# A step of the weight decode is issued behind a slot's last first product, and in the last certain slot the first block's rows are read and normalized earlier

## The chip, the cores and the metric

One core of a Trainium2 chip runs the whole program. The metric is the device time of one execution in microseconds (us). Three runs of the kernel before took 1637.15, 1641.0 and 1641.97 us; their median is 1641.0 us.

## What is computed

Three parts follow each other: attention over keys and values pooled by eight, a mixture of eight experts with one expert per token, and a gated layer behind an RMS norm. Only the second and third matter here.

```python
logits = x @ w_gate                       # mixture: one expert per token
expert_idx = np.argmax(logits, axis=1)
h = np.maximum(xe @ w1[e], 0.0)           # xe: the tokens of expert e
out[mask] = gate_w[mask, None] * (h @ w2[e])
...
rms = np.sqrt(np.mean(x * x, axis=-1, keepdims=True) + 1e-06)
xn = x / rms * rms_g                      # gated layer
g = xn @ w_gate
silu = g * (1.0 / (1.0 + np.exp(-g)))
return (silu * (xn @ w_val)) @ w_out
```

There are 4608 tokens of width 512; an expert has 1024 hidden columns, the gated layer 1536. Its three weight matrices come as 64-bit floats, 18 *units* in all, each of two halves.

## The kernel before

**Slots.** Behind the attention the tokens are worked off in slots of 256 tokens of one expert (`body`, line numbers as in the profile). Slots 0 to 17 are certain to be needed; from slot 18 on each stands in a branch. A slot has two stages. Stage 1 (`stage1`, L572) makes eight first products, two to each of four PSUM banks `p_0` to `p_3`; behind each second one ScalarE rectifies the bank into `hh` (L575) and VectorE makes the remainder `hl` (L576). Then eight transposes (`xpose`, L605) prepare the tokens of the next slot, whose casts are L610 on ScalarE and L611 on VectorE. Stage 2 (`stage2`, L1058) makes the second products in one or two halves of 128 tokens: eight matmuls with `hh` and `w2h`, eight with `hh` and `w2l`, eight with `hl` and `w2h`. A half ends with the scaled result `ys` (L1069 or L1067), a sum of squares (L1070) and a store to `y_d` (L1073).

**New experts.** Where a slot begins a new expert, `change` and `change_half` split its weights within branches: `w2h` on ScalarE and `w2l` on VectorE (L149 and L150, 128x1024) behind the slot's first product, `w1h` and `w1l` (128x512) one slot earlier, one half of them behind the first product with number 4.

**The decode.** Beside the slots the 18 units are turned from 64-bit words into a high and a low 32-bit part. `unit_load` (L964) fetches a half of a unit into the tile `us`, of which there are two buffers. `unit_steps` gives the five steps of one half: step 1 a square on ScalarE (L983, it waits for the load and writes `ub`), step 2 (L986, L988), step 3 (L992, L994), step 4 (L997, L998) and step 5 (L1002) on VectorE.

**Order.** Nothing is scheduled automatically: each engine runs its instructions in the order in which the code issues them. The loop over the slots builds a table `fill` from places to steps, by `put_in`. Places 0 to 7 are behind the first product of that number, place 8 is behind the transposes and casts for the next slot, place 9 behind the first half of stage 2, place 10 behind the second. For slots 1 to 17 the five steps of a unit's first half stand at 2, 7, 7, 8, 8 and those of the second half at 9, 9, 10, 10, 10.

**The first block of the gated layer.** In slot 17 `ready` (place 8) reads the first 256 rows of `y_d` into a buffer of `us` (L1114); `norm_0` (place 10) normalizes them: a copy on GpSimd (L1141), two squares on ScalarE (L1139), twelve small steps on VectorE (L1120 to L1130) and two scalings (L1147). `turn_0` then transposes them on TensorE (L1155) ahead of slot 18, and ScalarE and VectorE take them out of PSUM (L1159, L1160).

Of the kernel before, what the change touches and what calls it, by code (L numbers as in the profile page):

```python
# [83 lines left out]
def fused(ctx: ExitStack, tc: tile.TileContext, q, k, v, moe_w_gate, moe_w1, moe_w2,  # L84
# [12 lines left out]
    NU = 18  # L97
# [502 lines left out]
    def xpose(s, c):  # L600

        px_ = px(c)
        for d in range(2):
            for z in range(2):
                nc.tensor.transpose(px_[:, d, 128 * z:128 * z + 128],  # L605
                                    xg[s][:, z, (2 * c + d) * 128:(2 * c + d) * 128 + 128], ident)
        if c and not s:
            nc.scalar.copy(out=lg0, in_=xg[0][:, :, DM:XW])
        hi, lo = (x[:, 2 * c:2 * c + 2] for x in xts[s])
        nc.scalar.copy(out=hi, in_=px_)  # L610
        nc.vector.tensor_tensor(out=lo, in0=px_, in1=hi, op=ALU.subtract)  # L611
        if c and s:
            gate_of(s)
# [347 lines left out]
    def unit_load(u, j):  # L961
        src, kk = unit_src(u, j)
        t = us_p.tile([128, 2 * DM + 2], I32 if wide else F32, tag="us", name="us")[:, 0:1024 if wide else 512]
        nc.sync.dma_start(out=t.rearrange("p (k n) -> p k n", k=kk), in_=src)  # L964
        ust[u, j] = t
# [41 lines left out]
    def unit_store(u):  # L1007
        if stored(u):
            for i, x in enumerate(held.pop(u)):
                nc.sync.dma_start(out=scr[u - EARLY, i], in_=x.bitcast(F32))  # L1010

    def gather(s):
        xg[s], xts[s] = xgs[s % 2], xhl[s % 2]
        for z in range(2):
            nc.gpsimd.indirect_dma_start(
                out=xg[s][:, z], out_offset=None, in_=x_d[:, :],
                in_offset=bass.IndirectOffsetOnAxis(ap=idx_g[:, z, s:s + 1], axis=0))
# [57 lines left out]
    def body(s, fill, f0=0):  # L1075

        last = s + 1 == NSLOT

        def put(place):
            for f in fill.get(place, ()):  # L1080
                f()

        for f in range(f0, 8):
            stage1(s, f)
            if f == 0 and s > 1:
                change(s, 1)
            if f == 4 and s and not last:
                change_half(s + 1, 0)
            put(f)
        if s and not last:  # L1090
            if s > 1:
                xpose(s + 1, 0)
                xpose(s + 1, 1)
            change(s + 1, 0)
            if s + 2 < NSLOT:
                gather(s + 2)
        xts.pop(s)
        put(8)
        soon(s + 1)
        stage2(s, 0, fill)  # L1100
        put(9)
        if s > 1:
            with tc.If(flag(s, HALF) > 0, preferred_fallthrough_block=True):
                stage2(s, 1)
        else:
            stage2(s, 1, fill)
        put(10)
# [99 lines left out]
    for s in range(SURE):  # L1207
        fill = {}

        def put_in(place, f):  # L1210
            fill.setdefault(place, []).append(f)

        if s == 0:
            for place, fs in tail.items():
                for f in fs:
                    put_in(place, f)
        if s == 1:
            put_in(0, lambda: gather(2))
            put_in((1, 2), lambda: xpose(2, 0))
            put_in((1, 3), lambda: xpose(2, 1))  # L1220
        for place, f in late:
            put_in(place, f)
        a = unit_steps(s, 0)
        b_ = unit_steps(s, 1)
        for place, f in zip((2, 7, 7, 8, 8) if s else [(0, 4)] * 5, a):
            put_in(place, f)
        if s + 1 < NU:
            put_in(9 if s else (0, 6), lambda s=s: unit_load(s + 1, 0))
        else:
            put_in(8, ready)  # L1230
        for place, f in zip((9, 9, 10, 10, 10) if s else [10] * 5, b_):
            put_in(place, f)
        if s + 1 == NU:
            put_in(10, norm_0)
        late = [(3, lambda s=s: unit_store(s))]
        if s + 1 < NU:
            late.append((3, lambda s=s: unit_load(s + 1, 1)))
        body(s, fill, 0 if s else 3)
        if s == 0:
            sctx.close()  # L1240
            vctx.close()
            psm = mctx.enter_context(tc.tile_pool(name="ps_m", bufs=1, space=PSUM))
            p1[:] = [psm.tile([128, 2, T], F32, name=f"p1_{i}") for i in range(4)]
# [187 lines left out]
```

## Time and profile before

| what | value |
|---|---|
| profiled execution, its own time | 1643.06 us |
| its span | 1641.3 us |
| median of three runs | 1641.0 us |
| TensorE busy, share of the span | 97% |
| VectorE / ScalarE / GpSimd busy | 51% / 30% / 16% |
| mean granted clock of TensorE | 0.983 |

The profiled execution's time is the span from its first to its last instruction and 1.8 us around it. The profile names TensorE PE (its weight loads PEld), VectorE DVE, ScalarE ACT, GpSimd POOL and SyncE SP; SPq is SP's issue of transfers. In a timeline a row has the start in us from the span's start, the length, engine, line, operation, the tiles and the count of merged instructions; a bracket gives the idle time of the engine ahead of the row and what ended it.

### The profile page before, as it was taken

The numbers are of one execution on the slowest core, as the hardware profiler recorded it, in microseconds if no ns is written. First come the engines' busy times: TensorE is split into PE (matmuls) and PEld (weight loads), VectorE is DVE, ScalarE is ACT, GpSimd is POOL, SyncE is SP. The second block draws the span as 40 slices with busy tenths as digits, with TensorE's granted clock in tenths as the row PEclk, the third lists the DMA queues.
The fourth block names the chain that finished last, engine by engine and source line by source line (L and its number), as shares of the span: only waits on it lengthen the run. The fifth ranks groups of instructions, "written<-read, shape, count | busy, mean of one in ns | idle before, by whom it ended". The sixth has DMA issues, their size and how long they took to land. (4 is left out here: it accounts for less than half of the span.)

```text
span 1641.3 us, 26444 instructions
## 1 busy us (share of the span) xinstructions
PE 1592.7 (97%) x9397; PEld 1377.7 (84%) x9399; DVE 836.6 (51%) x1717; ACT 488.9 (30%) x940; POOL 265.2 (16%) x362
## 2 busy tenths in 40 slices
PE   8999999999999998999999999999999999999997
PEld 6898889987998887889888888888888888888886
DVE  5688975778667785224433433334343333443222
ACT  3455633545334452222212112121211212122121
POOL 4687751011101110103000000000000000000000
PEclk9999999999999998999999999999999999999999
DMA  8977726486647464119201000010010001000000
GB/s 232 251 180 166 208 88 199 164 275 239 209 151 239 151 202 132 47 35 326 54 13 32 20 13 26 14 39 13 20 33 13 26 14 39 14 0 26 1 27 13
DMA packets 123515, 161.95 MB, mean 99 GB/s; under 512 B 36560, under 2 KB 85072, under 8 KB 123360
## 3 DMA queue, kind: packets, MB, share of 16 engines
q1 hardware_dynamic: 111328, 124.00, 26.1%
q0 software_dynamic: 11776, 35.91, 7.0%
q8 instruction: 77, 1.26, 0.3%
q14 instruction: 78, 0.64, 0.1%
q10 hardware_dynamic: 256, 0.13, 0.0%
HBM read 116.93 MB, written 43.08 MB: 97 GB/s over the span
## 5 line engine op out<-in xcount | busy, mean ns | idle before, releaser
L1328 DVE SCALAR_TENSOR_TENSOR th<-th,g 128x512 f32<-128x512 f32 (+1 forms) x120 | 76.1, 634 | 471.3 <-ACT th L1327 471.3
L1325 PE MATMUL g<-xh,rl 128*128 128x512 f32 (+1 forms) x576 | 217.3, 377 | 0.0
L1324 PE MATMUL g<-xl,rh 128*128 128x512 f32 (+1 forms) x576 | 217.3, 377 | 0.0
L1323 PE MATMUL g<-xh,rh 128*128 128x512 f32 (+1 forms) x576 | 217.2, 377 | 0.0
L1327 ACT ACTIVATE th<-g 128x512 f32<-128x512 f32 (+1 forms) x120 | 66.8, 557 | 463.4 <-PE g L1325 463.4
L1354 POOL DMA_INDIRECT out_dram<-o,tk x36 | 34.7, 965 | 815.7 <-ACT o L1353 788.9
L1349 PE MATMUL po<-rl,a 128*128 128x512 f32 x360 | 140.3, 390 | 1.6 <-DMA rl<-scr 1.6
L1348 PE MATMUL po<-rh,a 128*128 128x512 f32 x360 | 140.2, 389 | 0.0
L1350 PE MATMUL po<-rh,a 128*128 128x512 f32 x360 | 140.0, 389 | 0.0
L1323 PEld LDWEIGHTS g<-xh,rh 128*128 128x128 f32 x576 | 108.4, 188 | 20.3
L1324 PEld LDWEIGHTS g<-xl,rh 128*128 128x128 f32 x576 | 108.4, 188 | 20.3
L1325 PEld LDWEIGHTS g<-xh,rl 128*128 128x128 f32 x576 | 108.4, 188 | 19.9
L149 ACT CAST a<-th 128x512 fp32r<-128x512 f32 (+1 forms) x120 | 69.3, 578 | 167.2 <-DVE th L1329 167.2
L150 DVE TENSOR_TENSOR a<-th,a 128x512 fp32r<-128x512 f32 (+1 forms) x120 | 76.7, 639 | 77.3 <-ACT a L149 77.3
L1323 PE MATMUL g<-xh,uh 128*128 128x512 f32 (+1 forms) x288 | 108.7, 378 | 1.7 <-DVE th L1329 1.7
L1324 PE MATMUL g<-xl,uh 128*128 128x512 f32 (+1 forms) x288 | 108.6, 377 | 0.0
L1325 PE MATMUL g<-xh,ul 128*128 128x512 f32 (+1 forms) x288 | 108.6, 377 | 0.0
L572 PE MATMUL p<-xh,w1h 128*128 128x256 f32 x672 | 107.9, 283 | 0.6
L572 PE MATMUL p<-xh,w1l 128*128 128x256 f32 x672 | 106.9, 281 | 0.0
L572 PE MATMUL p<-xl,w1h 128*128 128x256 f32 x672 | 106.6, 280 | 0.0
L576 DVE SCALAR_TENSOR_TENSOR hl<-p,hh 128x512 fp32r<-128x512 f32 x84 | 56.9, 689 | 86.1 <-ACT hh L575 63.7
L572 PEld LDWEIGHTS p<-xh,w1h 128*128 128x128 f32 x672 | 92.7, 190 | 3.8 <-issue 1.1
(307 smaller groups left out, 3007.6 us busy)
## 6 DMA issues: line engine op xcount, KB each, us to landing
st<-in_moe_w_dram SPq DMA_DIRECT2D x64, 512.0 KB
y_d<-ys SPq DMA_DIRECT2D x39, 257.0 KB
v<-in_v_dram SPq DMA_DIRECT2D x32, 288.0 KB
y<-y_d SPq DMA_DIRECT2D x68, 128.0 KB
x_d<-x SPq DMA_DIRECT2D x16, 520.0 KB
k<-in_k_dram SPq DMA_DIRECT2D x16, 512.0 KB
q<-in_q_dram SPq DMA_DIRECT2D x14, 512.0 KB
scr<-uh SPq DMA_DIRECT2D x13, 512.0 KB
```

What stands on the lines that cost most here:

```text
L149: nc.scalar.copy(out=hi, in_=src)
L150: eng.tensor_tensor(out=lo, in0=src, in1=hi, op=ALU.subtract)
L572: nc.tensor.matmul(a, lhsT=w[d][:, fs], rhs=x[:, d], start=j + d == 0, stop=j == 2 and d == 3)
L576: nc.vector.scalar_tensor_tensor(out=lo, in0=bank, scalar=0.0, in1=hi, op0=ALU.max, op1=ALU.subtract)
L1323: nc.tensor.matmul(g[:, j], lhsT=wh[:, sl], rhs=hi[:, d], start=d == 0, stop=False)
L1324: nc.tensor.matmul(g[:, j], lhsT=wh[:, sl], rhs=lo[:, d], start=False, stop=False)
L1325: nc.tensor.matmul(g[:, j], lhsT=wl[:, sl], rhs=hi[:, d], start=False, stop=d == 3)
L1327: nc.scalar.activation(out=th, in_=g[:, 0], func=AF.Tanh, scale=0.5)
L1328: nc.vector.scalar_tensor_tensor(out=th, in0=th, scalar=1.0, in1=g[:, 0], op0=ALU.add, op1=ALU.mult)
L1348: nc.tensor.matmul(po, lhsT=a[:, 0, tsl], rhs=wh[:, sl], start=c == 0, stop=False)
L1349: nc.tensor.matmul(po, lhsT=a[:, 0, tsl], rhs=wl[:, sl], start=False, stop=False)
L1350: nc.tensor.matmul(po, lhsT=a[:, 1, tsl], rhs=wh[:, sl], start=False, stop=c == NC2 - 1)
```

## The change

In slots 1 to 16 step 1 of a unit's first half goes from place 2 to place 7. In slot 17 the first half's steps stand at places 2, 2, 3, 3, 3, the read of the first block at 4 and its norm at 9, ahead of what the second half has there; the second half's steps stand at 7, 7, 9, 9, 10.

```diff
-        for place, f in zip((2, 7, 7, 8, 8) if s else [(0, 4)] * 5, a):
+        end = s + 1 == NU
+        for place, f in zip((2, 2, 3, 3, 3) if end else (7, 7, 7, 8, 8) if s else [(0, 4)] * 5, a):
             put_in(place, f)
         if s + 1 < NU:
             put_in(9 if s else (0, 6), lambda s=s: unit_load(s + 1, 0))
         else:
-            put_in(8, ready)
-        for place, f in zip((9, 9, 10, 10, 10) if s else [10] * 5, b_):
+            put_in(4, ready)
+            put_in(9, norm_0)
+        for place, f in zip((7, 7, 9, 9, 10) if end else (9, 9, 10, 10, 10) if s else [10] * 5, b_):
             put_in(place, f)
-        if s + 1 == NU:
-            put_in(10, norm_0)
```

Three places show what it moves. The first is ScalarE in an ordinary slot, between the rectifications of the four banks. Before:

```order
L575 ACTIVATE hh<-p_0_3386 128x512
L983 ACTIVATE ub<-us 128x512
L575 ACTIVATE hh<-p_1_3387 128x512
L1023 TENSOR_LOAD row_i
L1027 COMPARE_AND_BRANCH
```

The square L983 stood behind the first bank's rectification. Now ScalarE has, at the end of the same slot's stage 1:

```order
L575 ACTIVATE hh<-p_2_3388 128x512
L575 ACTIVATE hh<-p_3_3389 128x512
L983 ACTIVATE ub<-us 128x512
L610 CAST xh_3109<-px 128x512 x2
L595 ACTIVATE gdf<-gdf 128x16
```

It stands behind the fourth bank and ahead of the casts for the next slot. The second place is VectorE at the end of slot 17. Before, the second half's steps 3 to 5 stood behind the slot's last scaling L1067, and the norm behind them:

```order
L1067 TENSOR_SCALAR ys_3120<-y,gates 128x512
L1103 UNCONDITIONAL_BRANCH x2
L992 SCALAR_TENSOR_TENSOR uh_9281<-ub,ua 128x512
L994 TENSOR_SCALAR ua<-uh_9281 128x512
L997 TENSOR_SCALAR ub<-us 128x512
L998 SCALAR_TENSOR_TENSOR ub<-us,ub 128x512
L1002 SCALAR_TENSOR_TENSOR ul_9282<-ub,ua 128x512
L1120 TENSOR_SCALAR nm_93<-nm_93 128x2
```

Now the norm's last small steps and its scalings L1147 come first:

```order
L1128 SCALAR_TENSOR_TENSOR nm_93<-nm_93 128x2
L1130 SCALAR_TENSOR_TENSOR nm_93<-nm_93 128x2
L1147 TENSOR_SCALAR y_9438<-y_9438,nm_93 128x512 x2
L992 SCALAR_TENSOR_TENSOR uh_9281<-ub,ua 128x512
L994 TENSOR_SCALAR ua<-uh_9281 128x512
L997 TENSOR_SCALAR ub<-us 128x512
L998 SCALAR_TENSOR_TENSOR ub<-us,ub 128x512
L1023 TENSOR_LOAD row_i
L1103 COMPARE_AND_BRANCH
L1067 TENSOR_SCALAR ys_3120<-y,gates 128x512
```

The norm went ahead of steps 3 to 5 and of the last scaling. The third place is ScalarE at the end of slot 17. Before:

```order
L1070 ACTIVATE y,ys_3119<-y,gates 128x512
L983 ACTIVATE ub<-us 128x512
L1023 TENSOR_LOAD row_i
L1103 COMPARE_AND_BRANCH
L1070 ACTIVATE y,ys_3120<-y,gates 128x512
L1103 UNCONDITIONAL_BRANCH x2
L1139 ACTIVATE sq_9673,nm_93<-y_9552 128x512
```

Now:

```order
L1069 ACTIVATE ys_3119<-y,gates 128x512
L1070 ACTIVATE y,ys_3119<-y,gates 128x512
L1139 ACTIVATE sq_9614,nm_93<-y_9438 128x512
L1139 ACTIVATE sq_9616,nm_93<-y_9438 128x512
L1023 TENSOR_LOAD row_i
L1103 COMPARE_AND_BRANCH
L1070 ACTIVATE y,ys_3120<-y,gates 128x512
```

The norm's two squares stand behind the first half instead of the second, and the square L983 of the second half has left this place.

## Rows read from the trace of the kernel before

**Rows 1.** The page's part 1: busy us (share of the span) xinstructions.

```profile
PE 1592.7 (97%) x9397; PEld 1377.7 (84%) x9399; DVE 836.6 (51%) x1717; ACT 488.9 (30%) x940; POOL 265.2 (16%) x362
```

**Rows 2.** Timeline of PE, slot 8, a slot without a stall.

```profile
408.23 0.63 PE L572 MATMUL p<-xh,w1h 128*128 128x256 f32 x4
...
419.43 1.03 PE L605 MATMUL px<-cc,both 128*128 128x128 f32 x8
420.22 2.11 PE L1058 MATMUL y<-w2h,hh 128*128 128x512 f32 x8
...
431.50 0.63 PE L572 MATMUL p<-xh,w1h 128*128 128x256 f32 x4
```

**Rows 3.** Timeline of PE, stage 2 of slot 5.

```profile
343.03 0.72 PE L1058 MATMUL y<-w2h,hh 128*128 128x512 f32 x2
346.65 2.99 PE L1058 MATMUL y<-w2h,hh 128*128 128x512 f32 x6 [2.90 <-ACTq L1027]
...
360.29 0.64 PE L572 MATMUL p<-xh,w1h 128*128 128x256 f32 x4
```

**Rows 4.** Timeline of PE, stage 2 of slot 7.

```profile
390.58 0.70 PE L1058 MATMUL y<-w2h,hh 128*128 128x512 f32 x2
...
395.65 2.07 PE L1058 MATMUL y<-w2h,hh 128*128 128x512 f32 x4 [1.83 <-ACT hh L575]
```

**Rows 5.** Timeline of PE, stage 2 of slot 12.

```profile
508.71 0.71 PE L1058 MATMUL y<-w2h,hh 128*128 128x512 f32 x2
511.32 0.73 PE L1058 MATMUL y<-w2h,hh 128*128 128x512 f32 x2 [1.90 <-ACTq L1027]
...
524.18 0.63 PE L572 MATMUL p<-xh,w1h 128*128 128x256 f32 x4
```

**Rows 6.** Timeline of PE, from the end of slot 17 through slot 18's stage 1.

```profile
643.94 2.12 PE L1155 MATMUL px<-cc,y 128*128 128x128 f32 x8 [6.56 <-issue]
...
658.90 1.04 PE L605 MATMUL px<-cc,both 128*128 128x128 f32 x8
```

**Rows 7.** Windows: length, busy us by engine, then PEclk, DMA share, GB/s.

```profile
345.90:352.70 6.80, 6.05 (x14) 4.57 (x15) 6.33 (x13) 2.75 (x6) 0.40 (x1) 0.50 0.99 296
...
209.00:216.00 7.00, 6.68 (x60) 6.69 (x61) 6.35 (x22) 2.20 (x5) 5.50 (x8) 1.00 0.20 79
```

**Rows 8.** Timeline of ACT, the squares of both unit halves in slot 5.

```profile
345.45 0.67 ACT L983 ACTIVATE ub<-us 128x512 f32<-128x512 f32 x1 [2.72 <-DMA us<-in_moe_w_gate_dram]
...
358.98 0.68 ACT L983 ACTIVATE ub<-us 128x512 f32<-128x512 f32 x1 [2.68 <-DMA us<-in_moe_w_val_dram]
```

**Rows 9.** Timeline of DVE, slot 5 (first two rows) and slot 7.

```profile
341.63 4.63 DVE L150 TENSOR_TENSOR w2l<-st,w2h 128x1024 fp32r<-128x1024 f32 x4 [0.35 <-ACT w2h L149]
346.17 1.28 DVE L576 SCALAR_TENSOR_TENSOR hl<-p,hh 128x512 fp32r<-128x512 f32 x2
...
387.24 4.63 DVE L150 TENSOR_TENSOR w2l<-st,w2h 128x1024 fp32r<-128x1024 f32 x4 [0.33 <-ACT w2h L149]
...
393.85 2.50 DVE L150 TENSOR_TENSOR w1l<-st,w1h 128x512 fp32r<-128x512 f32 x4
```

**Rows 10.** Timeline of PE, 209 us, a single wait.

```profile
209.32 1.73 PE L446 MATMUL av<-vbd,ptsb 96*128 96x146 f32 x12 [0.96 <-DVE x L477]
```

**Rows 11.** Timeline of several engines, end of slot 17.

```profile
633.02 0.20 ACT L1070 ACTIVATION_READ_ACCUMULATOR y<-y,gates 128x1 f32 x1
633.09 0.39 SPq L1114 DMA_DIRECT2D y<-y_d  x1
...
636.91 0.19 POOL L1141 COPY tk<-y 128x2 int32<-128x2 int32 x1 [15.58 <-DMA y<-y_d]
...
638.93 0.59 ACT L1139 ACTIVATE sq<-y 128x512 f32<-128x512 f32 x1
...
640.93 0.16 DVE L1120 TENSOR_SCALAR nm<-nm 128x2 f32<-128x2 f32 x1
...
643.35 0.89 DVE L1147 TENSOR_SCALAR y<-y,nm 128x512 f32<-128x512 f32 x2
```

## The prediction

> **What bounds the kernel.** I read the page first: TensorE is busy for 97% of the span, and no other engine for more than 51% [rows 1]. So a microsecond is won only where TensorE waits or where its clock is low. The waits of TensorE, listed with what ended them, are few; between 200 and 760 us the long ones that this change can touch are in stage 2 of slots 5, 7 and 12 and at the turn from slot 17 to slot 18. I then read TensorE's timeline there and held it against a slot without a stall.
>
> The measure is slot 8 [rows 2]. From its first product to its transposes it takes 419.43 - 408.23 = 11.20 us, the eight transposes take 0.79 us, and stage 2 with both halves takes 431.50 - 420.22 = 11.28 us, so 1.88 us for eight matmuls, 0.47 for two, 5.64 for a half.
>
> - Slot 5: 360.29 - 343.03 = 17.26 us [rows 3], 5.98 too many. The wait is 2.90 of it; the other 3.08 are clock: for 6.8 us behind the wait the granted clock is 0.50 [rows 7], 1.2 instead of 2.4 GHz.
> - Slot 7: from 390.58 [rows 4] to slot 8's first row at 408.23 [rows 2], 17.65 us, 6.37 too many, of which one wait is 1.83 [rows 4].
> - Slot 12: 524.18 - 508.71 = 15.47 us, 4.19 too many, with a wait of 1.90 [rows 5].
> - The turn: a wait of 6.56 us, then eight transposes and slot 18's stage 1 in 658.90 - 643.94 = 14.96 us [rows 6], where slot 8 needs 0.79 + 11.20 = 11.99, so 2.97 of low clock: 6.56 + 2.97 = 9.53.
>
> Together 5.98 + 6.37 + 4.19 + 9.53 = 26.07 us that TensorE loses there. The question is how much of it the change gives back.
>
> **Slots 5, 7 and 12.** All three begin a new expert. In slot 5 ScalarE, between the first and second rectification, is held for 2.72 us at the square L983, until the unit's load has landed at 345.45 [rows 8]; the three rectifications behind it are late, and TensorE, which already has the first two matmuls of stage 2 behind it, waits for them. With L983 behind the fourth rectification nothing that waits for a load stands ahead of them any more, and the wait goes. What is late next is VectorE, which must finish `w2l` and then make `hl`:
>
> - Slot 5: `w2l` ends at 341.63 + 4.63 = 346.26, four `hl` of 0.64 follow (1.28 for two) [rows 9], to 348.8; two matmuls and a half, 0.47 + 5.64, give 354.9. Without any wait stage 2 would end at 343.03 + 11.28 = 354.3. So 0.6 us stay.
> - Slot 7: the next slot begins a new expert too. `w2l` ends at 391.87, two `hl` 1.28, four `w1l` 2.50 [rows 9], two `hl` 1.28: 396.9; plus 0.47 and 5.64 is 403.0, against 390.58 + 11.28 = 401.9 without a wait. That leaves 1.2 if ScalarE and VectorE come forward with TensorE. They may not entirely: the load of slot 5's second unit half, for which ScalarE waits until 358.98 [rows 8], is issued behind the new expert's transfers and does not come forward. At worst the 5.4 us won in slot 5 are missing again in slot 7; at best nothing is. I take 0.4 of it, since there is a whole slot (slot 6) between for the two engines, which TensorE outlasts, to catch up: 1.6 us stay.
> - Slot 12: I have no row for its `hl`; what stays is between 0 and slot 5's 0.6. I take 0.3.
>
> The square itself costs nothing elsewhere: 0.67 us [rows 8] on an engine that is busy for 30%. But its wait now has other work behind it on ScalarE: the two casts L610 for the next slot, the gate's L595 and the scaling L1069. In slot 5 the load landed at 345.45, 3.2 us behind the last first product (343.03 - 0.79 = 342.24) [rows 3, 8]; the casts are wanted only when stage 2 is over, 11.28 us later or 5.64 in a slot with one half. In the 13 other slots from 1 to 16 TensorE loses little or nothing today at this place, so I cost the move at zero there, and the cover is that stage 2.
>
> Does the clock come back with the waits? At 209.32 TensorE had waited 0.96 us [rows 10], and over the 7 us from 209.0 the granted clock is 1.00 [rows 7]. The waits left here are single pieces of at most 0.8 us. I take it that the clock stays up.
>
> **The turn.** The read of the first block moves from behind the casts to place 4, behind the first half's decode, whose seven VectorE instructions are now ahead of the second `hl`; TensorE wants that `hl` only in the last third of the half, over 4 us after stage 1. The read took from 633.09 to 636.91, 3.8 us [rows 11]; issued some 7 us earlier it has landed when ScalarE is through with the first half at 633.2 (633.02 + 0.20) [rows 11]. SP's queue behind it holds the branch flags and the stores of stage 2, wanted later. Then: two squares, between 2 x 0.59 = 1.2 and 640.93 - 638.93 = 2.0; I take 1.5, as each is followed by the read of its sum: 634.7. Twelve small steps, 643.35 - 640.93 = 2.42: 637.1. Two scalings, 0.89 together: 637.6 and 638.0 [rows 11]. TensorE ends stage 2 at 643.94 - 6.56 = 637.38 [rows 6]. So the first transposes wait 0.2 us and those of the other 128 rows until 638.0: with the hand-overs 0.7 us stay of 9.53, and after so short a wait no clock is lost. Behind the norm, VectorE's scaling L1067 of the second half comes about 3 us later than today, and so the store and ScalarE's L1159; TensorE needs the PSUM banks of these only in slot 18's transposes and stage 2, 11 us on.
>
> **The sum.** Given back: 26.07 - (0.6 + 1.6 + 0.3 + 0.7) = 22.9 us. From slot 18 on everything moves forward as it is. The profiled execution took 1643.06 us, 0.13% above the median of 1641.0; against it the sum is 1620.2, and against the median **1618.1 us**.
>
> **Rivals.**
> - *Short waits still halve the clock.* Slot 5 keeps 0.6 us of waits, slot 7 1.6 us in three pieces. Each place that loses the clock again costs up to the 3.08 us of slot 5. For it: in slot 7 two waits in a row, each under 2 us, were enough. Against it: the 0.96 us at 209.32. One place gives 1621.2, all three of slot 5, slot 7 and the turn 1618.1 + 9.2 = 1627.3. The Trainium skill, "TensorE: Matmul & The Clock Gate", section "A second HAM failure mode: psum-queue depth-cycling", tells of a kernel whose clock swung although TensorE idled only briefly between groups of matmuls. By that rule this rival holds; the row at 209.0, with one wait and the full clock, does not bear it out.
> - *The second half's load comes late in slot 17.* Its L983 now stands ahead of the casts L610 and L1069; the trace says only that it had landed when ScalarE came to it, at the end of the first half. If it lands only then, the square, two casts and the gate push the squares back by some 2.5 us, the turn waits about 3 us and keeps its 2.97 us of low clock: 1618.1 + 5.2 = 1623.3.
> - *Only the turn is won.* If the three stalls are not the load's but come from ScalarE being late for other reasons, the change does not do there what it says: 9.53 - 0.7 = 8.8, so 1632.2. Against it: the row of L983 names the load [rows 8].
> - *Slower.* The square at place 7, held by its load, keeps the next slot's casts back, and TensorE stands at the next slot's first product. It decides where the load lands more than 5.64 - 2.4 = 3.2 us behind the last first product in a slot with one half, or 8.9 in one with two. To end at 1646, 22.9 + 4.9 us would have to be lost, 1.7 us in each of 16 slots. Slot 5, with its 3.2 us, is at the edge for a short slot, but it is a long one.
>
> **How the numbers follow.** A measurement of this kernel can tell about 0.3%, 4.9 us, from no change. The forecast has 0.60, the clock 0.20, the late load 0.08, the turn alone 0.05: all faster, 0.93 together. For a gain that is eaten up almost entirely, by several of these at once, 0.04; for slower 0.03. The range takes in the clock's rival, to 1627; at the low end all 26.07 us come back, 1614.9, and the runs before spread by 2 to 4 us: 1612. It leaves out the turn alone, no change and slower, 0.12 together.
>
> **What would show it.** In the profile of the changed kernel stage 2 of the three slots lasts 11.9, 12.9 and 11.6 us, the transposes L1155 wait under 1 us, and there is no window at clock 0.50 between 340 and 700 us. L983 stands behind the fourth rectification and still waits for its load in slot 5. Wrong would be a wait of TensorE ahead of a slot's first product, stage 2 of slot 7 above 15 us, or a wait of several us at L1155 for L1147.

## The result, and the profile after

The changed kernel takes 1619.85 us (median of 4 runs, 1618.34 to 1620.74); before, 1641.28 us (4 runs). The ratio is 0.9874, with an interval of 0.9856 to 0.9892. The profiled execution took 1619.92 us with a span of 1618.1, against 1643.06 and 1641.3: 23.2 us of span to account for.

On the page TensorE now works 98% of the span [rows 1]; its busy time fell by 10.3 us although its instructions are as many as before, so they ran faster.

```profile
PE 1582.4 (98%) x9397; PEld 1369.2 (85%) x9399; DVE 834.5 (52%) x1717; ACT 486.8 (30%) x940; POOL 263.2 (16%) x362
```

TensorE's timeline of the changed kernel, stage 2 of slots 5, 7 and 12 from its first row to the next slot's first product, answers to [rows 3 to 5]:

```profile
343.05 2.12 PE L1058 MATMUL y<-w2h,hh 128*128 128x512 f32 x8
...
354.34 0.64 PE L572 MATMUL p<-xh,w1h 128*128 128x256 f32 x4
...
385.42 2.11 PE L1058 MATMUL y<-w2h,hh 128*128 128x512 f32 x8
...
389.23 2.40 PE L1058 MATMUL y<-w2h,hl 128*128 128x512 f32 x8
392.24 2.13 PE L1058 MATMUL y<-w2h,hh 128*128 128x512 f32 x8 [0.60 <-issue]
...
397.93 0.63 PE L572 MATMUL p<-xh,w1h 128*128 128x256 f32 x4
...
497.96 2.12 PE L1058 MATMUL y<-w2h,hh 128*128 128x512 f32 x8
...
509.43 0.64 PE L572 MATMUL p<-xh,w1h 128*128 128x256 f32 x4
```

Where the wait of 2.90 us stood in slot 5, the eight matmuls follow each other. ScalarE's timeline of the same slot shows why: the fourth rectification is done when the square begins to wait, and the square still waits for its load, now 0.96 us [rows 8]:

```profile
342.08 1.09 ACT L575 ACTIVATE hh<-p 128x512 fp32r<-128x512 f32 x2 [0.32 <-ACTq L1027]
344.14 0.67 ACT L983 ACTIVATE ub<-us 128x512 f32<-128x512 f32 x1 [0.96 <-DMA us<-in_moe_w_gate_dram]
```

The end of slot 17, on several engines, answers to [rows 6, 11]:

```profile
611.82 0.39 SPq L1114 DMA_DIRECT2D y<-y_d  x1
613.90 0.67 ACT L983 ACTIVATE ub<-us 128x512 f32<-128x512 f32 x1 [1.87 <-DMA us<-in_moe_w_out_dram]
616.13 0.19 POOL L1141 COPY tk<-y 128x2 int32<-128x2 int32 x1 [11.27 <-DMA y<-y_d]
618.60 0.69 ACT L1069 ACTIVATE ys<-y,gates 128x512 f32<-128x512 f32 x1 [1.70 <-PE y L1058]
619.84 0.60 ACT L1139 ACTIVATE sq<-y 128x512 f32<-128x512 f32 x1
623.95 0.88 DVE L1147 TENSOR_SCALAR y<-y,nm 128x512 f32<-128x512 f32 x2
624.53 1.46 PE L1155 MATMUL px<-cc,y 128*128 128x128 f32 x8 [0.43 <-PE y L1058]
625.75 0.72 PE L572 MATMUL p<-xh,w1h 128*128 128x256 f32 x4
...
637.15 1.04 PE L605 MATMUL px<-cc,both 128*128 128x128 f32 x8
```

The block's rows have landed at 616.13, ScalarE squares them at 619.84, straight behind the first half's sum, and the transposes wait 0.43 us instead of 6.56. Windows over the places where the clock had fallen (length; busy us by engine; then PEclk, DMA share, GB/s) answer to [rows 7]. Before, in slots 7 and 12 and at the turn, the granted clock was 0.50:

```profile
393.70:400.50 6.80, 4.97 (x12) 3.80 (x12) 6.61 (x13) 3.35 (x7) 0.00 (x0) 0.50 1.04 395
513.20:516.60 3.40, 3.40 (x10) 2.62 (x9) 3.30 (x7) 0.44 (x1) 0.00 (x0) 0.50 0.78 260
639.50:649.70 10.20, 5.76 (x27) 5.61 (x28) 6.09 (x21) 2.65 (x8) 2.78 (x4) 0.50 0.70 145
```

After, it is 1.00 in all four places:

```profile
345.90:352.70 6.80, 6.80 (x30) 5.45 (x30) 5.37 (x13) 0.61 (x2) 0.98 (x1) 1.00 0.93 335
382.00:399.00 17.00, 16.40 (x90) 13.34 (x89) 15.82 (x29) 9.21 (x20) 4.16 (x4) 1.00 0.87 283
509.00:516.00 7.00, 7.00 (x59) 6.91 (x58) 5.86 (x10) 2.46 (x6) 0.41 (x2) 1.00 0.83 250
620.00:650.00 30.00, 29.57 (x184) 25.96 (x183) 13.28 (x36) 8.58 (x20) 4.21 (x6) 1.00 0.42 99
```

The account of the 23.2 us, each line from the start of a place to the next row behind it:

| place | before | after | won |
|---|---|---|---|
| up to slot 1's first product | 242.72 | 242.71 | 0.0 |
| slot 5, stage 2 | 17.26 | 354.34 - 343.05 = 11.29 | 5.97 |
| slot 7, stage 2 | 17.65 | 397.93 - 385.42 = 12.51 | 5.14 |
| slot 12, stage 2 | 15.47 | 509.43 - 497.96 = 11.47 | 4.00 |
| the turn, wait through slot 18's stage 1 | 6.56 + 14.96 = 21.52 | 0.43 + 637.15 - 624.53 = 13.05 | 8.47 |
| all else from slot 1 to slot 21's end | | | -1.77 |
| behind slot 21 | 905.07 | 903.69 | 1.38 |

Slot 21's end is the start of the next row less its wait, 736.23 before and 714.41 after, so that slots 1 to 21 took 493.51 and 471.70 us; what lies behind is the span less that end. TensorE's first row behind slot 21, before and then after:

```profile
739.80 0.58 PE L1323 MATMUL g<-y0t,uh 128*128 128x256 f32 x1 [3.57 <-ACTq L1244]
```

```profile
717.88 0.58 PE L1323 MATMUL g<-y0t,uh 128*128 128x256 f32 x1 [3.47 <-ACTq L1244]
```

The wait there is the same. The 1.38 us come from the clock behind it: the windows 737 to 747 before and 716 to 726 after have 0.66 and 0.83.

```profile
737.00:747.00 10.00, 7.20 (x40) 7.20 (x41) 0.84 (x2) 1.28 (x5) 3.80 (x8) 0.66 0.38 110
```

```profile
716.00:726.00 10.00, 8.12 (x57) 8.12 (x58) 1.65 (x4) 1.17 (x3) 4.72 (x9) 0.83 0.48 147
```

### The profile page after: what moved, and what is told of

It reads as the page before. It is cut to its first block, busy times and chain, and to the rows that moved or that the text cites. A ratio compares the mean times of both kernels' runs of the same rounds, so it can differ in the third digit from the quotient of the medians.

```text
span 1618.1 us, 26443 instructions
## 1 busy us (share of the span) xinstructions
PE 1582.4 (98%) x9397; PEld 1369.2 (85%) x9399; DVE 834.5 (52%) x1717; ACT 486.8 (30%) x940; POOL 263.2 (16%) x362
```

## The experiments

The experiments ran on three later occasions: the first four rows of the table on the first, the next four on the second, the last three on the third. The attention ahead of slot 1 then took 3 to 13 us longer than in the first two profiles, by an amount that changed from run to run, and the kernel before had medians of 1647.77, 1647.74 and 1644.59 us. So each kernel's time is held against before on its own occasion, and the traces by slots 1 to 21 alone, from slot 1's first product to slot 21's end as above. The kernel before, profiled once more on the third, gives 490.45 us. Each figure for the slots is from one profile, and two profiles of one kernel differ by up to 3 us. By them the change won 21.8 us in the slots the first time and 17.4 us later.

| kernel | median us | ratio to before | interval | slots 1 to 21, us |
|---|---|---|---|---|
| ordinary slots alone | 1635.07 | 0.9920 | 0.9899 to 0.9942 | 483.25 |
| slot 17 alone | 1640.60 | 0.9965 | 0.9948 to 0.9983 | 481.28 |
| square on other data | 1635.25 | 0.9926 | 0.9904 to 0.9949 | 478.98 |
| square at place 5 | 1630.53 | 0.9891 | 0.9867 to 0.9915 | 472.94 |
| the change again | 1628.72 | 0.9894 | 0.9860 to 0.9928 | 473.05 |
| second load first | 1626.30 | 0.9865 | 0.9835 to 0.9895 | 468.73 |
| before, filled | 1647.34 | 0.9997 | 0.9978 to 1.0017 | 485.80 |
| first load late | 1655.81 | 1.0043 | 1.0016 to 1.0069 | 499.81 |
| read early alone | 1633.18 | 0.9923 | 0.9900 to 0.9945 | 477.98 |
| norm early alone | 1629.33 | 0.9896 | 0.9872 to 0.9920 | 470.38 |
| second load first, again | 1623.88 | 0.9868 | 0.9845 to 0.9891 | 468.32 |

### The cause of the three stalls: the square on other data

The kernel before, but the square of a first half reads the bank that ScalarE has just rectified:

```diff
         def s1():
-            nc.scalar.activation(out=b_, in_=word(1).bitcast(F32), func=AF.Square)
+            src = word(1).bitcast(F32)
+            if j == 0 and u:
+                src = hh[:, 0:2].rearrange("p f t -> p (f t)").bitcast(F32)
+            nc.scalar.activation(out=b_, in_=src, func=AF.Square)
```

> The kernel before, with the square of each unit's first half at place 2 as it was, but reading the first rectified bank instead of the loaded words: same engine, place, size and output, no wait for the load. The decoded weights of the gated layer are then not the reference's. Theory (the wait for the load is the cause): the three stalls go though the order is unchanged; stage 2 of slots 5, 7 and 12 lasts at most 12.0, 13.1 and 12.1 us, 1626.3 to 1628.5 us in all. Rival (ScalarE is late there for other reasons, and the square's own 0.67 us or its place does it): waits of 1.8 to 2.9 us stay, and the time stays within 3 us of 1641.

Measured: stage 2 of slots 5, 7 and 12 lasts 11.28, 12.66 and 11.28 us. In slot 5, ScalarE (its square is L986 here) and TensorE (L1061) show:

```profile
349.94 0.63 ACT L986 ACTIVATE ub<-hh 128x512 f32<-128x512 f32 x1
350.48 0.58 ACT L575 ACTIVATE hh<-p 128x512 fp32r<-128x512 f32 x1
```

```profile
351.64 2.11 PE L1061 MATMUL y<-w2h,hh 128*128 128x512 f32 x8
```

The square stands where it stood before, runs as long, and costs nothing. What stalled TensorE was the wait for the load, not the square nor a late ScalarE. The rival is out. In time this kernel is 12.5 us below before, just short of the 12.8 to 15 us that the expected times stand for; the turn is as it was.

### How far it depends on the place: place 5

```diff
-        for place, f in zip((2, 2, 3, 3, 3) if end else (7, 7, 7, 8, 8) if s else [(0, 4)] * 5, a):
+        for place, f in zip((2, 2, 3, 3, 3) if end else (5, 7, 7, 8, 8) if s else [(0, 4)] * 5, a):
```

> The changed kernel with the square of slots 1 to 16 at place 5, behind the third rectification and ahead of the fourth. Theory (only what stands behind the square waits for the load): only the fourth bank is late. In slot 5 the load lands at 344.1 to 345.5, so the bank at 345.3 to 346.7, and TensorE wants it at 343.05 + 6 x 0.235 = 344.5: a wait of 0.9 to 2.2 us; in slot 12 about 0.2 us, in slot 7 none. If the clock falls only behind waits of over 1.8 us, 1620.5 to 1622 us; if also behind shorter ones, up to 1625. Rival (any square between the rectifications costs what it cost at place 2): stage 2 of the three slots is back at 17.3, 17.7 and 15.5 us, 1633 or more.

Measured in slot 5, on ScalarE and on TensorE:

```profile
355.52 0.67 ACT L983 ACTIVATE ub<-us 128x512 f32<-128x512 f32 x1 [1.81 <-DMA us<-in_moe_w_gate_dram]
```

```profile
356.72 0.73 PE L1058 MATMUL y<-w2h,hh 128*128 128x512 f32 x2 [1.25 <-ACT hh L575]
```

Six of the eight matmuls run, and the two that need the fourth bank wait 1.25 us, inside the expected 0.9 to 2.2. Slot 7 waits 0.58 and 0.71 us and slot 12 0.65 us, more than expected. Only what stands behind the square is late, and by the load's lateness less the lead that it has over TensorE. None of these waits brought the clock down (1.00 from 354 to 364, 396 to 412 and 510 to 525). The kernel is 17.2 us below before, the change, on the second occasion, 19.0.

### The two parts alone

Ordinary slots alone, with slot 17 as before:

```diff
-        for place, f in zip((2, 2, 3, 3, 3) if end else (7, 7, 7, 8, 8) if s else [(0, 4)] * 5, a):
+        for place, f in zip((2, 7, 7, 8, 8) if end else (7, 7, 7, 8, 8) if s else [(0, 4)] * 5, a):
...
-            put_in(4, ready)
-            put_in(9, norm_0)
+            put_in(8, ready)
...
-        for place, f in zip((7, 7, 9, 9, 10) if end else (9, 9, 10, 10, 10) if s else [10] * 5, b_):
+        for place, f in zip((9, 9, 10, 10, 10) if s else [10] * 5, b_):
...
+        if end:
+            put_in(10, norm_0)
```

> Only the square of slots 1 to 16 moves from place 2 to place 7; slot 17 and the turn are as before. Theory (the square's wait for its load held back the rectifications): the three stalls go, stage 2 of slots 5, 7 and 12 lasts 11.3, 12.5 and 11.5 us as in the changed kernel, the turn keeps its wait of over 6 us. The changed kernel won 5.97 + 4.90 + 4.09 = 14.96 us there and lost some 1.8 us in short waits of other slots, so 1626.3 to 1628.1 us. Rival (the gain of the slots is spent at the turn or depends on slot 17's part): the turn's wait grows by what the slots win, and the time stays above 1636.

Slot 17 alone, with the square of the others at place 2:

```diff
-        for place, f in zip((2, 2, 3, 3, 3) if end else (7, 7, 7, 8, 8) if s else [(0, 4)] * 5, a):
+        for place, f in zip((2, 2, 3, 3, 3) if end else (2, 7, 7, 8, 8) if s else [(0, 4)] * 5, a):
```

> Only slot 17 is changed; the square of slots 1 to 16 stays at place 2. Theory (the two parts are independent): the stalls of slots 5, 7 and 12 stay at 17.3, 17.7 and 15.5 us, the turn's wait falls to about 0.4 us with no low clock behind it: 8.6 us won there, 9.9 with the shorter stretch of low clock behind the last slot: 1631.4 to 1632.7 us. Rival (slot 17's gain needs the earlier loads that the other part brings): a wait of 2 us or more stays at the turn, and the time is 1635 or more.

Measured: 12.7 us and 7.2 us below the median of before, where 13.2 to 15 and 8.6 to 9.9 were expected. The turn behaved as expected both times: with the slots alone it waits 6.57 us, with slot 17 alone 0.29. Two things in the slots did not.

With the ordinary slots alone, slots 5 and 12 last 11.28 us in stage 2, but slot 7 lasts 14.93. ScalarE had been held for 5.71 us at the end of slot 5, by the load of the unit's *second* half, and TensorE waits in slot 7:

```profile
372.98 0.69 ACT L983 ACTIVATE ub<-us 128x512 f32<-128x512 f32 x1 [5.71 <-DMA us<-in_moe_w_val_dram]
```

```profile
402.01 1.22 PE L1058 MATMUL y<-w2h,hh 128*128 128x512 f32 x4 [1.56 <-ACT hh L575]
```

With slot 17 alone, stage 2 of slots 5 and 12 lasts only 15.88 and 13.87 us where it lasted 17.26 and 15.47. In slot 12 the wait was as long as before (1.85 us, before 1.90 [rows 5]), but the clock stayed up. TensorE's row and its window:

```profile
519.14 0.73 PE L1058 MATMUL y<-w2h,hh 128*128 128x512 f32 x2 [1.85 <-ACTq L1027]
```

```profile
517.00:524.00 7.00, 4.96 (x21) 3.41 (x20) 6.25 (x11) 3.21 (x6) 0.95 (x2) 1.00 0.90 270
```

### What slot 7 still loses: the second half's load

The change once more, and the change with the second half's load at the head of the slot. In SP's queue it then stands ahead of the weight transfers, and also ahead of the two stores of the unit before (L1010), which had come between them:

```diff
         for f in range(f0, 8):
             stage1(s, f)
+            if f == 0:
+                put("head")
             if f == 0 and s > 1:
                 change(s, 1)
...
-            late.append((3, lambda s=s: unit_load(s + 1, 1)))
+            late.append(("head" if s else 3, lambda s=s: unit_load(s + 1, 1)))
```

> The changed kernel once more, unedited, beside the other runs of this call. In the run with the ordinary slots' move alone, the attention ran some 12 us longer and transfers came later, and slot 7 lost 3.7 us again. Theory (the gain of slot 5 is partly handed back in slot 7 when the second half's load, issued behind the new expert's weights, comes late): where that load makes ScalarE wait over 4 us at the end of slot 5, stage 2 of slot 7 is over 14 us; where it waits 2.4 us as in the first profile, about 12.5. Slots 5 and 12 at 11.3 to 11.7 us and a turn with a wait under 0.7 us in either case; 21 to 23 us faster than before in the first case less 2 to 4. Rival (slot 7's loss belongs to the kernel with slot 17 unchanged): slot 7 at 12.5 us whatever the load does.

> The changed kernel with the load of each unit's second half issued at the head of its slot, ahead of the new expert's weight transfers on SP's queue, instead of behind the first product with number 3. Theory (the second half's late load makes ScalarE and VectorE late in slot 6 and so in slot 7): the square of the second half in slot 5 waits under 0.5 us for its load, stage 2 of slot 7 is at most 12.2 us, and the kernel is as fast as the change or up to 1 us faster where transfers are quick, 2 to 5 us faster where they are late. Rival (the weights are pushed back instead: the queue waits for the buffer of the second half before it can issue them, and the transfers collide): the splits L149 and L150 of a later slot begin later, TensorE waits at a first product or stage 2, and the kernel is 1 us or more slower than the change.

> The changed kernel with the load of each unit's second half at the head of its slot, once more, for its interval. From the first full slot to the end of slot 21 it took 468.7 us, against 471.7 and 473.1 in the two profiles of the change. Theory (the late load in slots 5 to 7 is what the change still loses there): 468.5 to 470 us again, stage 2 of slot 7 at 12.4 us or less, and a time against before of 0.984 to 0.988. Rival (the difference of 3 to 4.3 us was chance): 471 to 474 us, and a ratio of 0.988 or more.

Measured: in the repeat of the unedited change slot 7 lasts 14.57 us in stage 2, so what happened with the ordinary slots alone has nothing to do with slot 17. The second half's square in slot 5 and TensorE in slot 7, in the change again:

```profile
363.69 0.68 ACT L983 ACTIVATE ub<-us 128x512 f32<-128x512 f32 x1 [5.11 <-DMA us<-in_moe_w_val_dram]
```

```profile
392.72 1.23 PE L1058 MATMUL y<-w2h,hh 128*128 128x512 f32 x4 [1.54 <-ACT hh L575]
```

The same square with the load first, again: it no longer waits for its load at all, but 0.78 us for VectorE.

```profile
361.69 0.68 ACT L983 ACTIVATE ub<-us 128x512 f32<-128x512 f32 x1 [0.78 <-DVE ul L1002]
```

Over all kernels with the square at place 7 and the first half's load where the change has it, the second half's wait for its load in slot 5 and slot 7's stage 2 go together in two groups: waits of 2.38, 2.54 and 3.56 us (the change, read early, norm early) with 12.51, 11.91 and 12.06; waits of 5.11 and 5.71 with 14.57 and 14.93. With the load first, stage 2 of slot 7 lasts 12.35 us, a little over the expected 12.2, and then 11.73. That the earlier load undoes slot 7's loss rests on one pair, 14.57 against 12.35 on the second occasion: on the third, read early and norm early lose little there without it, and the loss of the first profile had other parts. What delayed the load, the weights or the two stores, was not separated.

Slots 1 to 21 take 468.73 and 468.32 us, less than any other kernel here, 3.0 to 4.7 us less than the two profiles of the change and 2.1 us less than norm early alone on the same occasion. Against the repeat most of it is in slot 7; against the first profile it is in slots 6, 13 and 16. Against before the ratios are 0.9865 and 0.9868, and those of the change 0.9874 the first time and 0.9894 on the second occasion: lower twice, but with intervals that overlap. So the gain over the change stands in two traces against two, and is not shown by the times. The rival (the weights are pushed back) is not seen: slots 5 and 12 stay at 11.28 to 11.35.

### What the clock costs: filling the waits

The kernel before, with matmuls of zeros where TensorE waited:

```diff
         for n in range(24):
+            for _ in range({(5, 2): 12, (7, 2): 7, (7, 4): 7, (12, 2): 8}.get((s, n), 0) if z == 0 else 0):
+                nc.tensor.matmul(y, lhsT=ones, rhs=zero.unsqueeze(1).to_broadcast([128, 64, 8]), start=False, stop=False)
...
+            px_ = px(c)
+            for _ in range(0 if c else 29):
+                nc.tensor.matmul(px_.rearrange("p a b -> p (a b)"), lhsT=ones, rhs=zero.unsqueeze(1).to_broadcast([128, 64, 8]))
```

> The kernel before, with matmuls of zeros put into TensorE's stream at the four stalls (12, 14 and 8 in stage 2 of slots 5, 7 and 12, 29 ahead of the turn's transposes), somewhat shorter than the waits; nothing else is moved. Theory (about half of what the stalls cost is the clock that falls behind the wait): the waits' length stays but the clock stays at 1.00 in all four places: 3.1 us less in slot 5, 2.7 in slot 7, 2.1 in slot 12 and 3.0 at the turn, 10.9 us in all less than before. Rival (the clock falls for another reason than the idle engine, or zeros do not count): windows at clock 0.50 stay in these places and the time is within 2 us of before.

> The kernel before, unedited, for a profile beside the others of these calls, whose times of before were some 6 us above the first ones. Theory (the extra lies in the attention, whose transfers come later in these calls, and the loss in the slots is as it was): the first full slot starts some 8 us later than the 242.7 of the first profile, and from there to the end of slot 21 it takes 490 to 494 us, 21 to 24 more than the change. Rival (the stalls of before are smaller in these calls, since the clock does not fall behind each wait): 483 to 488 us, the waits as long as before but fewer windows at clock 0.50.

Measured: the time is that of before, 0.9997. The clock did what was expected; windows over slot 5 and over the turn, in before once more and then in the filled kernel:

```profile
354.00:364.00 10.00, 6.25 (x17) 4.61 (x17) 7.89 (x14) 3.24 (x7) 0.50 (x2) 0.66 0.75 246
...
645.00:663.00 18.00, 11.43 (x78) 11.20 (x78) 9.53 (x26) 5.09 (x12) 2.77 (x4) 0.81 0.58 120
```

```profile
354.00:364.00 10.00, 9.80 (x44) 6.23 (x43) 8.32 (x16) 3.42 (x7) 1.18 (x2) 1.00 0.90 290
...
642.00:660.00 18.00, 17.62 (x122) 13.56 (x121) 10.06 (x27) 5.70 (x13) 2.78 (x5) 1.00 0.58 119
```

But the gain was mis-sized. Before, once more, already lost less than in the first profile (its 490.45 us are 17.4 and 18.8 more than the two profiles of the change, where 21 to 24 was expected): stage 2 of slots 7 and 12 lasted 16.30 and 12.74 us, and behind the wait of 0.71 in slot 12 no clock was lost. Against it the filled kernel wins 3.32 us in slot 5, 1.39 in slot 7 and 1.89 over slots 17 and 18, loses 1.06 in slot 12, where the zeros take 1.91 us and the wait was 0.71, and 0.9 in other slots: 4.65 us over slots 1 to 21. Behind slot 21 it loses 2.05 again (907.03 against 904.98 us), where the longest wait within the gated layer is 3.12 instead of 1.74 us; why was not tried. Filling keeps the clock; the change, which removes the waits, is worth 12.8 to 14.1 us more in the same slots (485.80 against 473.05 and 471.70).

### How much the new place covers: the first half's load late

```diff
-            put_in(9 if s else (0, 6), lambda s=s: unit_load(s + 1, 0))
+            if not 0 < s < NU - 2:
+                put_in(9 if s else (0, 6), lambda s=s: unit_load(s + 1, 0))
...
+            if 0 < s < NU - 2:
+                late.append((2, lambda s=s: unit_load(s + 1, 0)))
```

> The changed kernel with the load of each unit's first half, in slots 2 to 16, issued in the slot itself behind the first product with number 2 instead of in the slot before behind the first half of stage 2. Theory (the square at place 7 holds back only the next slot's casts, so it may be late by stage 2 less 2.4 us of casts and gate: 8.9 us behind the last first product in a slot with two halves, 3.2 with one): in slots without weight transfers the load is issued 7 to 8 us ahead of the square and costs nothing; in slots with them (4, 5, 7, 8, 12, 15) it lands up to 10 us late, and TensorE waits at the next slot's first product, 2 to 7 us behind slots 4 and 15, under 3 us behind the others: 4 to 14 us slower than the change. Rival (the place covers any lateness, since stage 2 needs nothing of it): within 1.5 us of the change. The other side (a late square hurts as it did at place 2): waits in stage 2 of the same slot and over 20 us slower.

Measured: 27.1 us slower than the change on the same occasion (1655.81 against 1628.72), and slower than before. ScalarE and TensorE at the end of slot 4, which has one half:

```profile
343.60 0.67 ACT L983 ACTIVATE ub<-us 128x512 f32<-128x512 f32 x1 [8.10 <-DMA us<-in_moe_w_gate_dram]
344.17 1.06 ACT L610 CAST xh<-px 128x512 fp32r<-128x512 f32 x2
```

```profile
344.80 1.00 PE L572 MATMUL p<-xh,w1h 128*128 128x256 f32 x4 [3.51 <-ACT xh L610]
```

The mechanism is the one expected: the wait is at the next slot's first product, behind slots 4, 8 and 15, and stage 2 of slot 5 is untouched at 11.29. The size was low: behind each of the three waits, of 3.51, 3.23 and 3.28 us, the clock falls (0.79 in 344 to 360, 0.80 in 445 to 462, 0.77 in 610 to 630), and slots 5, 9 and 16, which follow them, become 4.38, 6.31 and 4.53 us longer than in the change again, on top of the waits (slot 9 also has a second wait of 1.28). It also gives the cover. TensorE could have begun at 344.80 - 3.51 = 341.29; the first product came 1.20 us after the landing; stage 1 ended at 334.65. So a load may land 341.29 - 1.20 - 334.65 = 5.4 us behind the last first product in a slot with one half. In the changed kernel slot 5's load, of the first halves the one for which the square waited longest, landed 344.14 - 342.26 = 1.9 us behind it.

### The turn: read early or norm early

Read early alone puts the norm back to place 10; norm early alone puts the read back to place 8:

```diff
             put_in(4, ready)
-            put_in(9, norm_0)
...
+        if end:
+            put_in(10, norm_0)
```

```diff
-            put_in(4, ready)
+            put_in(8, ready)
             put_in(9, norm_0)
```

> The changed kernel with the norm at place 10 again, behind both halves; the read stays at place 4. Theory (the turn's wait is the norm's chain behind the second half, not the read): the read lands over 10 us before it is wanted, and the turn still waits 5.5 to 6.6 us, with up to 3 us of low clock behind it: 5.5 to 9.5 us slower than the change. Rival (the read was the bound): the turn waits under 3 us, and the kernel is less than 4 us slower than the change.

> The changed kernel with the read at place 8 again, behind the casts for the next slot; the norm stays at place 9. In the kernel before the read was issued at 633.09, just when VectorE's last use of the buffer (L998) ended. Theory (what freed the read is the decode's earlier end, not its own place): the read is issued at the end of stage 1, some 1 to 2 us later than in the change, lands at least 3 us before ScalarE's squares, and the turn waits under 0.7 us: within 1 us of the change. Rival (the place of the read counts): it is issued behind the first half of stage 2, the squares wait for it, and the turn waits 2 us or more: 2 to 6 us slower than the change.

Measured with the read early alone, on ScalarE and TensorE:

```profile
627.13 0.59 ACT L1139 ACTIVATE sq<-y 128x512 f32<-128x512 f32 x1
...
631.58 2.12 PE L1155 MATMUL px<-cc,y 128*128 128x128 f32 x8 [6.00 <-issue]
```

and with the norm early alone, on SP, GpSimd, ScalarE and TensorE:

```profile
622.05 0.39 SPq L1114 DMA_DIRECT2D y<-y_d  x1
625.84 0.19 POOL L1141 COPY tk<-y 128x2 int32<-128x2 int32 x1 [12.05 <-DMA y<-y_d]
...
628.19 0.60 ACT L1139 ACTIVATE sq<-y 128x512 f32<-128x512 f32 x1
...
632.67 1.46 PE L1155 MATMUL px<-cc,y 128*128 128x128 f32 x8 [0.21 <-PE y L1058]
```

With the read early alone the turn waits 6.00 us and slots 1 to 21 take 7.6 us more than with the norm early alone (477.98 against 470.38), and 6.3 and 4.9 us more than in the two profiles of the change, where 5.5 to 9.5 was expected. The medians, 1633.18 and 1629.33, differ by less, since the time outside the slots differs too: slot 1 begins at 245.66 and 252.16 us. With the norm early alone the turn waits 0.21 us, no more than in the change, and the read has landed 2.35 us before the squares, a little less than the 3 expected. So the read's own place is worth nothing here. The buffer is free in time: VectorE's last use of it (L998) ends at 619.91, and the read is issued at 622.05, where before it was held until 633.09. That the decode's steps at 2, 2, 3, 3, 3 do this follows from the order; they were not put back by themselves.

## Why the prediction was right, step by step

The forecast was 1618.1 us; measured were 1619.85, and in the profiled execution 1619.92 against a forecast of 1620.2. Its main cause and its places are shown by the runs; the sum is right to some extent by luck, because errors cancel (+0.7 in the four places, -1.8 in the other slots, +1.4 behind them), and on the second occasion the same change gave 19.0 us instead of 21.4.

- **Slot 5** (0.6 us were to stay): nothing stayed, 11.29 against 11.28. The step that failed took the end of `w2l`, 346.26, as fixed. VectorE came forward as well: in the changed kernel, on VectorE, the split begins at 339.74, not at 341.63 [rows 9], and the first `hl` stand at 344.28.

```profile
339.74 4.62 DVE L150 TENSOR_TENSOR w2l<-st,w2h 128x1024 fp32r<-128x1024 f32 x4
344.28 1.28 DVE L576 SCALAR_TENSOR_TENSOR hl<-p,hh 128x512 fp32r<-128x512 f32 x2
```

- **Slot 7** (1.6 were to stay): 12.51 - 11.28 = 1.23. The bounds from nothing to 5.4 us missing again were the right worry: in two other runs, with the second half's load later, 3.3 and 3.7 us are missing. The pieces were not as told: `w1l` ahead of the last `hl` costs 2.40 - 2.03 = 0.37, and the wait of 0.60 ahead of the second half has no engine as its releaser.
- **Slot 12** (0.3): 0.19. **The turn** (0.7): 0.43 of wait, 0.43 more in the transposes (1.22 instead of 0.79) and 0.20 in stage 1 (11.40 instead of 11.20), 1.06 in all. Given back in the four places: 23.58, predicted 22.9.
- **The move costs nothing elsewhere**: this term failed by 1.77 us. Slots 6, 13 and 16 became 0.55, 0.68 and 0.90 longer, slot 9 0.33 shorter. In slot 16 the second half's load comes in again: in the first profile its square was held for 2.85 us in slot 15 and slot 16's stage 2 lasted 12.46 us, in the repeat it did not wait for that load and stage 2 lasted 11.30. Before had this too, with 2.83 and 11.71. With the load first the square does not wait for it, and stage 2 of slot 16 lasts 11.29 and 11.28. The waits ahead of stage 2 in slots 6 and 13 (0.29 and 0.28 us) have no releaser in the trace; in the repeat of the change slot 6 has none. Each lies beside a branch. The Trainium skill, "Runtime: NRT & Kernel Launch", section "Instruction fetch mechanics", says that a taken branch can force a fetch of instructions before execution goes on; the trace does not show that as the cause here: in the view of the transfers one fetch of instructions starts at 392.10, when slot 7's wait of 0.60 us (391.64 to 392.24) has almost ended, and none falls into those of slots 6 and 13. The cause of the three stays open.
- **Behind slot 21** the prediction moved everything forward as it is. It became 1.38 us shorter, by the clock behind an unchanged wait, which about pays for the 1.77.
- **The clock's rival** (0.20) did not come: 1.00 in all four places, with waits of up to 0.60 us. Other runs go further: waits of 1.25 us (place 5), 1.54 (the change again) and 1.85 (slot 17 alone) kept the clock too. By the rule that the prediction set beside it from the Trainium skill, "TensorE: Matmul & The Clock Gate", section "A second HAM failure mode: psum-queue depth-cycling", short idle times between groups of matmuls make the clock swing; the trace of the changed kernel does not bear that out here.
- **The late second load in slot 17** (0.08) came in its first half: ScalarE waited 1.87 us for it, at 613.90. It cost nothing, because the squares wait anyway for the first half of stage 2, whose result ScalarE took at 618.60; casts behind the load were done by 615.5. The step that was wrong is that the casts push the squares.
- **The turn alone** is excluded by the square on other data and by the ordinary slots alone. **The slower rival** is a mechanism that exists: with the load late the kernel is slower than before. Its edge was set too near, at 3.2 us behind a short slot's stage 1, since it counted 2.4 us of square, casts and gate ahead of the next slot's first product; only the square and the first cast stand there, 1.20 us. It also set the 5.64 us of a half against a lateness that is counted from the last first product, and left out the eight transposes between (0.79). The edge is at 5.4.
- **The read at place 4** was credited with the turn together with the norm. The runs show that the norm's place does it alone, once the buffer is free.

## What to carry to other kernels

An instruction that waits for a transfer belongs behind whatever another engine needs from the same in-order engine, and ahead of the work with the longest cover; what it then holds back, and by how much it may be late, can be measured by making the transfer late. When one wait is removed, look at the next transfer in the same queue: here the second half's load, behind the weights and two stores in SP's queue, took back up to 3.7 us two slots later, and moving its issue to the head of the slot took the wait away. Here a wait cost its length and sometimes as much again in clock (2.90 and 3.08 us in slot 5); a sum for it should name both and give the clock part a range.

## What the runs showed of the hardware that was not expected

The clock's fall behind a wait is not settled by the wait's length. 1.90 us in slot 12 cost a stretch at 1.2 GHz in the first profile of before (granted clock 0.50 in 513.20 to 516.60, above), 1.85 us in the same place did not with slot 17 alone; and the wait behind slot 21, 3.57 us before and 3.47 after, was followed by a low stretch that cost 1.4 us more before than after. What decides between them was not tried. Nearly the same programs also ran up to 13 us apart ahead of slot 1: in the later profiles TensorE waits in one piece of 1.8 to 5.6 us between 178 and 195 us, which the first two do not have, while slots 1 to 21 of one kernel differ by up to 3 us.
